# Threshold attention and an ELU feed-forward layer on one core: the score matmuls of full blocks split by halves of the queries

## The chip, the cores and the metric

The kernel runs on one core of a Trainium2 chip. A core has TensorE (PE, matmuls into PSUM), VectorE (DVE), ScalarE (ACT), GpSimd (POOL) and SyncE (SP, which issues most DMAs), each with its own queue of instructions. PSUM has 128 partitions and eight banks of 512 float32 columns.

The metric is the device time of one execution in microseconds. The kernel before has a median of 1265.05 us in three runs, from 1264.96 to 1265.5 us.

## The reference

Batch 8, 8 heads, 576 positions, 64 channels per head; 4608 tokens of 512 channels then go through a layer of 2048 hidden channels. Everything is float32.

```python
scores = scale * np.matmul(q, k.transpose(0, 1, 3, 2))        # (8, 8, 576, 576)
thresh = np.max(scores, axis=-1, keepdims=True) - tau
scores = np.where(scores >= thresh, scores, -1000000000.0)
scores = scores - np.max(scores, axis=-1, keepdims=True)
attn = np.exp(scores)
attn = attn / (np.sum(attn, axis=-1, keepdims=True) + 1e-09)
out = np.matmul(attn, v)                                      # heads side by side: x (4608, 512)
h = x @ w_in
g = np.where(h > 0.0, h, np.exp(np.minimum(h, 0.0)) - 1.0)
return g @ w_out
```

## The kernel before

**Pairs of heads.** Two heads of a batch are one pair, 32 pairs in all. The transposed queries `qT` and keys `kT` of a pair hold head 0 in partitions 0 to 63 and head 1 in partitions 64 to 127, one column per position. A score matmul contracts the 64 channels of one head, so it uses 64 rows of PE's array; which rows follows from the partitions. The 576 queries are four full blocks of 128 (i = 0 to 3, `NC` = 4) and a tail of 64. The queries of a block are the matmul's stationary operand: they are loaded as weights, and come out as the partitions of the scores. The keys stream.

**Early pairs (0 to 3).** `scores` (L479) makes one block of a pair, both heads: for each half of the 576 keys (`HALF` = 288) and each head, one matmul at L493. For the tail (i = NC) it takes `qd`, in which both heads stand in one 128-row operand. `EARLY`, a list written out by hand, gives the order of all tasks up to about 250 us, from the first pairs to pair 8; an entry such as `sc.3` is a call of `scores`, and `wsc.4.0.1` one half of a call of `wide_scores`.

**All other pairs.** `wide_scores` (L751) makes two blocks of a pair, both heads, in one go: four score matrices of 128 by 576, which lie one after another in five PSUM banks (`wide[0]`, the tile `sc`). They are cut where banks end, into eight matmuls at L766, in the order of the tuple `order`: head, block, first column, columns. Head 0 and head 1 alternate, and at no time write the same bank. After one of them ACT copies a column to `seen` (L769). `on_banks` records which engine last touched which bank, and adds the waits that follow: the score matmuls wait for ACT and DVE, which still read the old scores; DVE's maximum (L773), ACT's exponential (L783) and DVE's mask (L787) wait for the matmuls.

**The tail.** `tails_and_values` (L790) makes the scores of the last 64 queries of a pair (L813) beside the first product with the values of the pair two before (L818). Both are matmuls of 64 rows by 64 columns. The rest of the value product follows at L826: 128 rows by 64 columns, one head in each half of the columns.

**The order.** From about 250 us on a planner in the program's builder sets the order. `on_pe(cost, f)` puts PE's work one after another and moves a clock by a fixed cost (2.15 us for `wide_scores`); `at(t, f)` puts the other engines' work at a time. For each pair: `tail_step`, and twice `wide_step` followed by 14 pieces of the feed-forward layer (`ffn_quarters(14)`: L1444 for the first product, L1584 for the second, both matmuls of 128 by 128). After the last pair only feed-forward work is left (L1444, L1958, L2020). The costs only order the work; at run time the engines wait for each other by semaphores.

Of the kernel before, what the change touches and what calls it, by code (L numbers as in the profile page):

```python
# [176 lines left out]
def kernel(  # L177
# [10 lines left out]
    nc = tc.nc  # L188
    PSUM = bass.MemoryType.PSUM
    P = 128  # L190
    B, H, S, D = q.shape
    DM, DF = moe_w_in.shape
    NC = S // P
    MAIN = NC * P
    TAIL = S - MAIN
    HALF = S // 2
# [274 lines left out]
    def vectors(pr):  # L471
        st = {x: small.tile([P, 2], FP32, name=x) for x in ("mx", "th", "su", "rs")}
        st["no"] = step_no[0]
        step_no[0] += 1
        st["sm"] = totals[:, step_no[0] % 6]
        return st


    def scores(pr, i, hs):  # L479
        qT, kT, qd = pairs[pr]  # L480
        if hs[0] == 0:
            open_steps[pr, i] = vectors(pr)
        st = open_steps[pr, i]
        scs = {}
        for h in hs:
            scs[h] = slots[slot_no[0] % 2]
            slot_no[0] += 1
        for a in range(2):
            for h in hs:
                k0 = a * HALF + (0 if h else TAIL)  # L490
                r, qs = (slice(h * D, (h + 1) * D), qT[:, i * P : (i + 1) * P]) if i < NC else (slice(0, P), qd)
                o = scs[h][:, a, :HALF]
                on_banks(nc.tensor.matmul(o, qs[r], kT[r, k0 : k0 + HALF], start=True, stop=True, skip_group_check=True), o)  # L493
        for h in hs:
            st[h] = scs[h]

# [222 lines left out]
    def on_banks(made, ap):  # L719

        ins, needed, starts = made.ins, [], [ap.offset % (5 * 512)]
        for step, n in ap.ap[1:-1]:
            starts = [s + step * k for s in starts for k in range(n)]
        engine = str(ins.engine)
        for x in sorted({b for s in starts for b in range(s // 512, (s + ap.ap[-1][1] - 1) // 512 + 1)}):
            others = [i for e, i in accesses.setdefault(x, []) if e != engine]
            needed += others
            if others and engine == str(nc.tensor.engine):
                accesses[x] = []
            accesses[x].append((engine, ins))  # L730
        needed += [i for y in after[0] for i in banked.get(y, {}).values() if str(i.engine) != engine and i not in needed]
        if doing[0]:
            banked.setdefault(doing[0], {})[engine] = ins
        for other in needed:
            tc.add_manual_dep(ins, other.name,
                              mybir.DependencyInfo(mybir.DependencyClass.Sync, mybir.DependencyReason.DATA), reason="bank")
        for e in (nc.tensor, nc.scalar, nc.vector):
            if str(e.engine) != engine:
                tc.declare_no_dep(ins, group=str(e.engine), keep=needed, reason="other banks")
        tc.add_to_no_dep_group(engine, ins)  # L740
# [5 lines left out]
    def open_step(pr, i, w):  # L746
        st = open_steps[pr, i] = vectors(pr)
        st["w"] = w
        return st

    def wide_scores(pr, half, parts=(0, 1)):  # L751

        qT, kT, _ = pairs[pr]
        for s in range(2) if parts[0] == 0 else ():
            i = 2 * half + s
            st = open_step(pr, i, turned_by[1 - s])
            for h in range(2):
                c = 2 * T + (2 * h + (s ^ h)) * S
                st["sc", h], st["e", h] = wide[0][:, c : c + S], st["w"][:, h * S : (h + 1) * S]
        order = (((0, 0, 0, 448), (1, 1, 0, 320), (1, 1, 320, 256), (0, 0, 448, 128)),  # L760
                 ((1, 0, 0, 256), (0, 1, 0, 384), (1, 0, 256, 320), (0, 1, 384, 192)))
        for h, s, c, n in [x for part in parts for x in order[part]]:
            i, r = 2 * half + s, slice(h * D, (h + 1) * D)
            k0 = c + (0 if h else TAIL)
            o = open_steps[pr, i]["sc", h][:, c : c + n]
            on_banks(nc.tensor.matmul(o, qT[r, i * P : (i + 1) * P], kT[r, k0 : k0 + n], start=True, stop=True,  # L766
                                      skip_group_check=True), o)
            if (h, s, c) == (1, 1, 0):
                on_banks(nc.scalar.copy(seen, o[:, :1]), o[:, :1])  # L769

# [286 lines left out]
    def early_tasks():  # L1057
# [128 lines left out]
        for n in range(per_seq):  # L1186
            pr, i = steps[n]
            hs = heads_of(i)
            masks_a.extend(("mask", n, h) for h in hs)
            job(("sc", n), "pe", lambda e, pr=pr, i=i, hs=hs: scores(pr, i, hs), ("prep", "k", pr, 0), ("copy", "k", pr),  # L1190
                ("prep", "q", pr, int(i > 0)) if i < NC else ("copy", "q", pr), ("sc", n - 1) if n else None, *[masks_a.pop(0) for _ in hs],
                soft=[("norm", n - 4, h) for h in heads_of(steps[n - 4][1])] if n > 3 else ())
# [75 lines left out]
        for z, (pr, what) in enumerate((pr, what) for pr in range(NPAIR, START) for what in ("tail", 0, 1)):  # L1268
            loc = {}
            if what == "tail":  # L1270
                v_ = pr - 2 if pr - 2 >= NPAIR else None
                need_v = [("landed", v_, x) for x in range(NB)] + [("v", v_)] if v_ else []
                job(("tail", pr), "pe", lambda e, pr=pr, v_=v_, loc=loc: loc.update(zip(("main", "outs"), tails_and_values(pr, v_))),
                    *ready_of[pr], *need_v, ("wsc", pr - 1, 1, 1) if pr > NPAIR else "t", *users, soft=steps_b[-4])
                sc_of = {(NC, 0): ("tail", pr)}
                if v_:
                    for part in (1, 0):
                        job(("main", v_, part), "pe", lambda e, part=part, loc=loc: loc["main"](part), ("tail", pr), ("main", v_, 1) if not part else None)
                        job(("outv", v_, part), "act|dve", lambda e, part=part, loc=loc: loc["outs"][part](e), ("main", v_, part))
                group_steps = [(NC, [0], 0)]  # L1280
            else:
                half = what
                for y in range(2):
                    job(("wsc", pr, half, y), "pe", lambda e, pr=pr, half=half, y=y: wide_scores(pr, half, (y,)),
                        ("wsc", pr, half, 0) if y else ("tail", pr) if not half else ("wsc", pr, 0, 1), *ready_of[pr], *users,
                        soft=() if y else steps_b[-4] + steps_b[-3])
                sc_of = {(2 * half + s, h): ("wsc", pr, half, s ^ h) for s in range(2) for h in range(2)}
                group_steps = [(2 * half, [0, 1], 1), (2 * half + 1, [1, 0], 0)]
# [91 lines left out]
    with tc.manual_schedule():  # L1380
# [319 lines left out]
        def wide_step(pr, half):  # L1700
            t = clock[0]
            on_pe(2.15, lambda: wide_scores(pr, half))
            e = t + 2.15
            for s in range(2):
                i = 2 * half + s
                at(e + 1.55 + 1.5 * s, lambda i=i: wide_bounds(pr, i), f"bound{i}")
                for h in range(2):
                    k = 2 * s + (h ^ s)
                    at(e + 0.75 * k, lambda i=i, h=h: wide_max(pr, i, h), f"max{i}{h}")
                    at(e + (1.6, 3.0, 4.7, 5.6)[k], lambda i=i, h=h: wide_exp(pr, i, h), f"exp{i}{h}")  # L1710
                    at(e + (3.0, 4.3, 6.5, 6.9)[k], lambda i=i, h=h: wide_mask(pr, i, h), f"mask{i}{h}")
                finish_of(pr, i, e + (5.1, 7.8)[s], e + (8.4, 10.5)[s])
            if pr + 1 < NP:
                at(e + 5.2, lambda: (prep_k if half else prep_q)(pr + 1), f"prep{half}")
                if not half:
                    at(e + 6.1, lambda: scale_q(pr + 1), "qscale")
                if half:
                    at(e + 6.1, lambda: copy_k(pr + 1), "kcopy")
                    if pr + 2 < NP:
                        at(e + 6.1, lambda: load(pr + 2, ("qm",), True), "loadq")  # L1720
                elif pr > START:
                    at(e + 6.1, lambda: load(pr + 1, ("km",), True), "loadk")
            extras(e + 0.3, e + 1.2, e + 4.2, e + 10.4, e + 12.0)
# [117 lines left out]
        x, y = spaces.popleft(), spaces.popleft()  # L1841
# [5 lines left out]
        a, z = B - 1, B  # L1847
# [281 lines left out]
```

## Time and profile before

| | |
|---|---|
| median of three runs | 1265.05 us (1264.96 to 1265.5) |
| span of the profiled execution, first to last instruction | 1263.4 us |
| PE busy | 1247.3 us, 7163 matmul records |
| PEld (weight loads) busy | 992.0 us, 7163 records |
| DVE, ACT, POOL busy | 1067.8, 584.5, 787.2 us |
| L766 matmul records | 896, 126.5 us busy |
| L493 matmul records with 64 rows | 128, 19.9 us busy |

The profiled execution's own time is known by its span, 1263.4 us; it is 1.65 us under the median of the runs.

How to read it. In a row of groups stand the line, engine, operation, the tiles written and read, the rows and columns of the array in use (64\*128 is 64 rows by 128 columns), the shape that streams, the count, the busy time, the mean duration of one in ns, and then the engine's idle time before them with what ended it. A float32 matmul of the source stands as two MATMUL and two LDWEIGHTS records. Matmuls overlap in the pipeline and their ends are modelled, so a stage is measured here from its first start to the first start of the next stage. In the timeline the first number is the start in us, the second the length, and xN merges N records. In rows of stretches stand the stretch, its length, and for PE, PEld, DVE, ACT and POOL (or those of the line asked for) the busy time and count; then PE's granted clock, the share of the DMA engines and GB/s.

### The profile page before, as it was taken

The page shows a single profiled execution, that of the slowest core. Times are in us where ns is not written, and L with a number is a line of the kernel's source. Part 1 is how long each engine was busy: PE and PEld are TensorE (multiplying, and loading weights), DVE is VectorE, ACT ScalarE, POOL GpSimd, SP SyncE. Part 2 cuts the span into 40 slices and gives each one's busy share as a digit, 9 for nine tenths or more (in the row PEclk, how much of TensorE's full clock was granted, in tenths as well). Part 3 has the DMA queues.
Part 4 walks back from the last instruction along what each step waited for, and adds up shares of the span by engine and source line. Part 5 has one row for each costly group of instructions (what it writes and reads, how often), then busy time and mean ns, then how long its engine had stood idle before and what let it go on. Part 6 is the DMA issues. An engine that isn't in the chain of part 4 may idle for free.

```text
span 1263.4 us, 22606 instructions
## 1 busy us (share of the span) xinstructions
PE 1247.3 (99%) x7163; PEld 992.0 (79%) x7163; DVE 1067.8 (85%) x2322; ACT 584.5 (46%) x1276; POOL 787.2 (62%) x1147
## 2 busy tenths in 40 slices
PE   8999999999999999999999999999999999999998
PEld 6776576588787787878788878778887888899998
DVE  6998989898889879898989888988988885777876
ACT  7987755463434435352625353444535260434130
POOL 5775545586576747574767657675757473675564
PEclk9999999999999999999999999999999999999999
DMA  8468898898989797989989897988898866444433
GB/s 225 147 181 244 217 265 241 241 299 218 263 210 270 217 247 218 263 239 241 238 228 260 225 264 201 274 217 244 216 271 228 236 213 229 156 136 150 142 109 110
DMA packets 332872, 277.71 MB, mean 220 GB/s; under 512 B 201296, under 2 KB 288336, under 8 KB 332752
## 3 DMA queue, kind: packets, MB, share of 16 engines
q1 hardware_dynamic: 331760, 275.73, 78.1%
q8 instruction: 57, 0.93, 0.3%
q10 hardware_dynamic: 992, 0.53, 0.1%
q14 instruction: 63, 0.52, 0.1%
HBM read 178.85 MB, written 97.32 MB: 219 GB/s over the span
## 4 chain that ended last, share of the span: by engine, by line
PE 90%; DVE 4%; DMA 2%; ACT 2%; issue 1%; SPq 0%; POOL 0%; DVEq 0%; ACTq 0%; POOLq 0%
PE f L1444 30%; PE f L1584 23%; PE sc L766 9%; PE sc L826 9%; PE f L1958 4%; PE f L2020 3%; PE f L953 2%; PE f L913 2%; PE sc L493 2%; PE sc L818 1%; PE sc L813 1%; DVE mx L773 1%; PE f L554 1%; PE sc L712 1%; PE f L885 1%
## 5 line engine op out<-in xcount | busy, mean ns | idle before, releaser
L773 DVE TENSOR_REDUCE mx<-sc 128x1 f32<-128x576 f32 x252 | 180.1, 746 | 41.1 <-PE sc L766 34.1
L779 POOL TENSOR_SCALAR th<-mx,ntau 128x2 f32<-128x2 f32 (+1 forms) x140 | 46.0, 329 | 189.9 <-DVE mx L773 189.8
L783 ACT ACTIVATE w_one<-sc,mx 128x576 f32<-128x576 f32 x140 | 100.7, 740 | 132.2 <-DVE mx L773 113.4
L766 PE MATMUL sc<-kT,qT 64*128 64x256 f32 (+5 forms) x896 | 126.5, 418 | 2.1 <-ACT xt L432 0.9
L787 DVE SCALAR_TENSOR_TENSOR w_one<-sc,th,w_one 128x576 f32<-128x576 f32 x140 | 109.9, 812 | 20.4 <-ACT w_one L783 19.7
L766 PEld LDWEIGHTS sc<-kT,qT 64*128 64x128 f32 x896 | 99.3, 186 | 35.4 <-issue 18.9
L1444 PE MATMUL f<-xt,sw 128*128 128x256 f32 x512 | 123.7, 384 | 1.3 <-DMA sw<-win_sums 0.8
L1444 PE MATMUL f<-x,w_in_sb 128*128 128x256 f32 x512 | 122.8, 382 | 0.0
L783 ACT ACTIVATE e<-sc,mx 128x576 f32<-128x576 f32 x112 | 82.7, 742 | 86.1 <-DVE mx L773 84.5
L1444 PE MATMUL f<-xt,w_in_sb 128*128 128x256 f32 x512 | 121.2, 379 | 0.5 <-DVE xt L1053 0.5
L501 POOL TENSOR_SCALAR w_one<-w_one,rs 128x576 f32<-128x576 f32 x115 | 89.4, 787 | 38.9 <-DVE rs L551 38.9
L640 DVE STREAM_TRANSPOSE x<-w_one 128x512 f32<-128x512 f32 (+1 forms) x140 | 99.9, 743 | 13.5 <-POOL w_one L501 7.6
L1444 PEld LDWEIGHTS f<-xt,sw 128*128 128x128 f32 x512 | 94.1, 190 | 20.2 <-issue 4.3
L1444 PEld LDWEIGHTS f<-x,w_in_sb 128*128 128x128 f32 x512 | 96.2, 190 | 16.1 <-ACT g L1505 3.6
L1444 PEld LDWEIGHTS f<-xt,w_in_sb 128*128 128x128 f32 x512 | 97.2, 190 | 14.0 <-ACT e L783 0.8
L787 DVE SCALAR_TENSOR_TENSOR e<-sc,th,e 128x576 f32<-128x576 f32 x112 | 87.6, 807 | 8.3 <-ACT e L783 7.9
L1584 PE MATMUL f<-w_out_sb,g 128*128 128x256 f32 x384 | 92.0, 382 | 0.0
L1584 PE MATMUL f<-w_out_sb,s 128*128 128x256 f32 x384 | 91.9, 382 | 0.0
L1584 PE MATMUL f<-t,s 128*128 128x256 f32 x384 | 90.7, 379 | 0.0
L1584 PEld LDWEIGHTS f<-w_out_sb,g 128*128 128x128 f32 x384 | 72.0, 190 | 12.2 <-issue 2.9
L1584 PEld LDWEIGHTS f<-w_out_sb,s 128*128 128x128 f32 x384 | 71.9, 190 | 12.0 <-issue 2.5
L1584 PEld LDWEIGHTS f<-t,s 128*128 128x128 f32 x384 | 73.0, 190 | 9.9
(344 smaller groups left out, 2887.6 us busy)
## 6 DMA issues: line engine op xcount, KB each, us to landing
there<-x SPq DMA_DIRECT2D x452, 144.0 KB, 3.8
wTb<-there SPq DMA_DIRECT2D x58, 576.0 KB, 6.2
wTa<-there SPq DMA_DIRECT2D x55, 576.0 KB, 4.3
sw<-win_sums SPq DMA_DIRECT2D x62, 384.0 KB, 4.2
t<-wout_sums SPq DMA_DIRECT2D x45, 512.0 KB, 5.2
there<-x SPq DMA_DIRECT2D x112, 80.0 KB, 1.9
wTb<-there SPq DMA_DIRECT2D x56, 160.0 KB, 3.8
wst<-in_moe_w_in_dram SPq DMA_DIRECT2D x16, 512.0 KB, 4.7
```

The source lines that it names most:

```text
L501: nc.gpsimd.tensor_scalar(wv, wv, st["rs"][:, h : h + 1], 1.0, ALU.mult, ALU.mult)
L640: nc.vector.transpose(x[:, :, c0 : c0 + nc_], src.rearrange("p (c g n) -> p g c n", c=nc_, n=T))
L766: on_banks(nc.tensor.matmul(o, qT[r, i * P : (i + 1) * P], kT[r, k0 : k0 + n], start=True, stop=True, skip_group_check=True), o)
L773: on_banks(nc.vector.tensor_reduce(st["mx"][:, h : h + 1], st["sc", h], axis=AX.XY if i == NC else AX.X, op=ALU.max, negate=True), st["sc" ...
L779: nc.gpsimd.tensor_scalar(st["th"][:, cs], st["mx"][:, cs], -1.0, ntau, ALU.mult, ALU.add)
L783: on_banks(nc.scalar.activation(st["e", h], st["sc", h], AF.Exp, bias=st["mx"][:, h : h + 1]), st["sc", h])
L787: on_banks(nc.vector.scalar_tensor_tensor(st["e", h], st["sc", h], st["th"][:, h : h + 1], st["e", h], ALU.is_ge, ALU.mult, accum_out=st[" ...
L826: on_banks(nc.tensor.matmul(o, vm[:, h, c], parts[part][:, g0:g1, h * (NC + 1) + c], start=False, stop=(c == NC - 1), skip_group_check=Tru ...
L1444: nc.tensor.matmul(loc["banks"][place], left[:, j], right[:, j], start=(begins and j == 0), stop=(j == 1), skip_group_check=True)
L1584: nc.tensor.matmul(place(m), lhs, rhs, start=(begins and v == 0), stop=(v == RU - 1), skip_group_check=True)
L1958: nc.tensor.matmul(loc["x"][place][:, :P], left[:, v], right[:, v], start=(begins and v == 0), stop=(v == 1), skip_group_check=True)
L2020: nc.tensor.matmul(loc[c][:, :HM], lefts(g, r, c, m)[:, v], rights(r, m)[:, v], start=(v == 0), stop=(v == RU - 1), skip_group_check=True)
```

## The change

In `scores` and `wide_scores` each matmul of a full block becomes two. The stationary operand is 64 queries in place of 128, and the output is the lower or the upper 64 partitions of the same columns of PSUM. The keys that stream are the same for both. The second follows right behind the first. The tail of `scores` keeps its one matmul of 128 rows. What is computed, and where it lies, stays the same.

```diff
@@ scores
-                o = scs[h][:, a, :HALF]
-                on_banks(nc.tensor.matmul(o, qs[r], kT[r, k0 : k0 + HALF], start=True, stop=True, skip_group_check=True), o)
+                for y in range(2 if i < NC else 1):
+                    oy = scs[h][y * D : (y + 1) * D, a, :HALF] if i < NC else scs[h][:, a, :HALF]
+                    on_banks(nc.tensor.matmul(oy, qs[r, y * D : (y + 1) * D] if i < NC else qs[r], kT[r, k0 : k0 + HALF], start=True, stop=True, skip_group_check=True), oy)
@@ wide_scores
             o = open_steps[pr, i]["sc", h][:, c : c + n]
-            on_banks(nc.tensor.matmul(o, qT[r, i * P : (i + 1) * P], kT[r, k0 : k0 + n], start=True, stop=True,
-                                      skip_group_check=True), o)
+            for y in range(2):
+                oy = o[y * D : (y + 1) * D]
+                on_banks(nc.tensor.matmul(oy, qT[r, i * P + y * D : i * P + (y + 1) * D], kT[r, k0 : k0 + n], start=True, stop=True,
+                                          skip_group_check=True), oy)
             if (h, s, c) == (1, 1, 0):
                 on_banks(nc.scalar.copy(seen, o[:, :1]), o[:, :1])
```

## The prediction

> **What bounds the kernel now.** I read the page first: its engine line, its slices and its chain.
>
> ```profile
> span 1263.4 us, 22606 instructions
> ...
> PE 1247.3 (99%) x7163; PEld 992.0 (79%) x7163; DVE 1067.8 (85%) x2322; ACT 584.5 (46%) x1276; POOL 787.2 (62%) x1147
> ...
> PEclk9999999999999999999999999999999999999999
> ...
> q8 instruction: 57, 0.93, 0.3%
> ...
> PE 90%; DVE 4%; DMA 2%; ACT 2%; issue 1%; SPq 0%; POOL 0%; DVEq 0%; ACTq 0%; POOLq 0%
> PE f L1444 30%; PE f L1584 23%; PE sc L766 9%; PE sc L826 9%; PE f L1958 4%; PE f L2020 3%; PE f L953 2%; PE f L913 2%; PE sc L493 2%; PE sc L818 1%; PE sc L813 1%; DVE mx L773 1%; PE f L554 1%; PE sc L712 1%; PE f L885 1%
> ```
>
> TensorE (PE) is busy for 99% of the span at the full granted clock, and 90% of the chain that ended last is PE. A busy PE does not say that it is full, so I then asked for stretches, for all engines, and in a second question for the score line L766 alone.
>
> ```profile
> 0.00:125.00 125.00, 116.75 (x880) 88.39 (x881) 106.15 (x235) 103.47 (x222) 78.34 (x123) 1.00 0.73 197
> 125.00:255.00 130.00, 128.15 (x624) 77.82 (x622) 117.02 (x251) 76.20 (x146) 70.37 (x101) 1.00 0.90 243
> 255.00:960.00 705.00, 704.53 (x3957) 567.03 (x3956) 619.00 (x1364) 310.40 (x681) 461.93 (x696) 1.00 0.89 241
> ```
>
> ```profile
> 0.00:125.00 125.00, 2.48 (x16) 1.83 (x16) 1.00 0.73 197
> 125.00:255.00 130.00, 22.34 (x144) 16.54 (x144) 1.00 0.90 243
> 255.00:960.00 705.00, 92.86 (x672) 73.87 (x672) 1.00 0.89 241
> 960.00:1071.00 111.00, 8.84 (x64) 7.04 (x64) 1.00 0.75 231
> ```
>
> From 255 to 960 us the first busy column (PE) has 704.53 of 705 us. The longest wait of PE on anything after 255 us is one of 0.8 us:
>
> ```profile
> PE f L1444 <- DMA sw<-win_sums: 0.8, 1, 0.8
> ```
>
> So a microsecond that a score stage gains or loses there moves the end by a microsecond. Before 255 us the other engines are on the chain too. Now the stage itself, in the timeline of PE:
>
> ```profile
> 406.67 2.21 PE L766 MATMUL sc<-kT,qT 64*128 64x448 f32 x16
> 408.81 1.99 PE L1444 MATMUL f<-xt,sw 128*128 128x256 f32 x8
> ...
> 421.24 0.45 PE L813 MATMUL sc<-kT,qT 64*64 64x288 f32 x1
> 421.25 0.43 PE L818 MATMUL sc<-wTa,vd 64*64 64x256 f32 x1
> 421.25 0.45 PE L813 MATMUL sc<-kT,qT 64*64 64x288 f32 x1
> 421.26 0.48 PE L818 MATMUL sc<-wTb,vd 64*64 64x320 f32 x1
> 421.51 0.38 PE L818 MATMUL sc<-wTa,vd 64*64 64x256 f32 x1
> ...
> 422.37 2.37 PE L826 MATMUL sc<-wTb,vm 128*64 128x320 f32 x16
> 424.58 1.90 PE L826 MATMUL sc<-wTa,vm 128*64 128x256 f32 x16
> 426.40 2.21 PE L766 MATMUL sc<-kT,qT 64*128 64x448 f32 x16
> 428.54 1.99 PE L1584 MATMUL f<-w_out_sb,g 128*128 128x256 f32 x8
> 430.37 1.89 PE L1584 MATMUL f<-t,g 128*128 128x256 f32 x8
> 432.10 1.89 PE L1584 MATMUL f<-w_out_sb,g 128*128 128x256 f32 x8
> ```
>
> Starts are what counts here, since ends are modelled. Eight matmuls in the source give 16 records: each float32 matmul runs as two passes. From 430.37 to 432.10 eight records of 256 columns take 1.73 us, 0.216 us each, so a pass streams a column in 0.844 ns.
>
> A stage of L766 lasts 408.81 - 406.67 = 2.14 us, and the next one, 428.54 - 426.40, the same. Each head's row group streams 448 + 128 + 384 + 192 = 1152 columns in two passes: 2304 x 0.844 = 1.944 us. Were the two heads taken in turn it would be 3.89 us, so they already run side by side and the 128 rows are full. What is left, 2.14 - 1.944 = 0.196 us, is the start of the stage. These rows split it (the first line of each pair of counts is minimum, median, maximum in ns):
>
> ```profile
> L766 PE MATMUL sc<-kT,qT x16: 269/402/640, 406.7 to 408.6; 64*128 64x320 f32 x4, 64*128 64x256 f32 x4, 64*128 64x448 f32 x2, 64*128 64x128 f32 x2
> L766 PE MATMUL sc<-kT,qT 64*128 64x448 f32 x2 | 1.0, 588 | 0.0
> L813 PE MATMUL sc<-kT,qT x8: 402/402/453, 421.2 to 422.0; 64*64 64x288 f32 x8
> ...
> L766 PEld LDWEIGHTS sc<-kT,qT 64*128 64x128 f32 x896 | 99.3, 186 | 35.4 <-issue 18.9 <-ACT seen L769 2.5 <-ACT xt L432 1.9
> ...
> L813 PEld LDWEIGHTS sc<-kT,qT 64*64 64x64 f32 x224 | 14.2, 132 | 12.9 <-issue 6.0 <-POOL u L1463 3.3 <-ACT xs L432 1.5
> ```
>
> Of the two 448-column passes the first takes 640 ns, so the second takes 2 x 588 - 640 = 536: the first waits 0.104 us for its 128 columns of weights, which nothing covers. The remaining 0.092 us is the change of array shape.
>
> **The change part by part.**
>
> *The streaming.* Each of the eight matmuls becomes two of half the queries. A tile of 64 by 64 streams the same keys, so 1152 columns in two passes, 1.944 us, on each of four tiles. If the four run side by side, the stage streams as long as before: nothing is gained and nothing lost. The trace shows four such tiles in the tail stage (L813 and L818): the four first starts lie within 421.24 to 421.26 us, and the stage lasts 422.37 - 421.24 = 1.13 us for 576 columns in two passes per tile, which is 0.972 us of streaming. In sequence it would be twice that.
>
> *The start of the stage.* The weights are 64 columns in place of 128. The L813 row gives that start: 453 - 402 = 0.051 us in place of 0.104. The tail stage has 1.13 - 0.972 - 0.051 = 0.107 us left, where the wide stage has 0.092: 0.015 us for the later starts of the third and fourth tile. New stage: 1.944 + 0.051 + 0.107 = 2.102 us, 0.038 us less. Bounds: 0.053 less if the late starts cost nothing; 0.023 less if the 0.015 us doubles with twice the passes. I take 0.038, since it is the measured stage plus streaming alone.
>
> *How often.* 896 records are 56 stages of L766. From 255 us on there are (672 + 64) / 16 = 46, all in the stretch where PE waits for nothing: 46 x 0.038 = 1.75 us. Before it lie (16 + 144) / 16 = 10, and they are longer:
>
> ```profile
> 121.31 2.52 PE L766 MATMUL sc<-kT,qT 64*128 64x448 f32 x16 [0.33 <-DVE w_one L787]
> ...
> 148.43 2.52 PE L766 MATMUL sc<-kT,qT 64*128 64x448 f32 x16
> ...
> L493 PE MATMUL sc<-x 64*128 64x288 f32 x64 | 10.0, 427 | 1.0 <-DVE w L537 0.8
> L493 PE MATMUL sc<-kT,qT 64*128 64x288 f32 x64 | 9.9, 428 | 1.1 <-DVE w L537 0.6 <-DVE w_one L537 0.5
> ...
> 72.37 1.20 PE sc L493 x8
> ...
> 180.25 5.97 DMA wTb<-there
> ```
>
> There the two halves of the stage are separate tasks, 2.52 against 2.21 us, and the second half starts anew, so the start is saved twice: 20 x 0.038 = 0.76 us. The 128 records of L493 with 64 rows are 16 stages of 8, each with one start: 0.61 us. These 1.37 us count only where the chain passes there. It does through many of them (the row at 72.37), but it also takes DMA steps of 6 us (180.25). I take two thirds, 0.9 us; the bounds are none and all.
>
> *What comes with it.* PE gets 1024 more LDWEIGHTS and 1024 more MATMUL records, 14% of its 14326. Queue q8, which carries instructions, grows from 57 packets by about 8; its share is 0.3%, and the cover is that they are fetched ahead. Were that gone, each would stop PE for its landing. The order of all engines stays as it was. The second half-matmul has no wait of its own, since it writes the bank that the first has just waited for. ACT's copy of one column (`seen`, L769) waits for both halves and, in 14 places, for an earlier instruction of ACT; ACT is 46% busy, so I cost that at nothing. The maxima, exponentials and masks read the same banks about 0.04 us earlier, and nothing is queued differently behind them.
>
> *The sum.* 1.75 + 0.9 = 2.65 us less. The profiled span of 1263.4 us lies 1.65 us under the median of the runs, 1265.05; what lies around the span stays. Forecast: 1265.05 - 2.65 = 1262.4 us. With the bounds: 46 x 0.023 = 1.1 us gained at least, 1264.0; at most (46 + 20 + 16) x 0.053 = 4.3 us, 1260.7.
>
> **The rivals.**
>
> *The early part gives nothing.* Only the 46 late stages count: 1.75 us, 1263.3, within 0.2% (2.53 us, about what a measurement of this kernel can tell from no change). For it speaks the 180.25 row; against it that PE is busy for 245 of the first 255 us.
>
> *Slower: passes start in the order of the program.* Then a matmul's second pass, on the same tile, holds back the next tile's first one. The stage is the sum over all 16 matmuls of one pass each, 4608 columns x 0.844 = 3.89 us, and the last pass, 0.16: 4.05 in place of 1.94 us of streaming, 56 x 2.1 = 118 us, 1383. It decides once a stage loses more than the 0.053 us of its start. Against it: by strict order the third start in the tail stage would lie one pass, 0.24 us, behind the first, and it lies 0.01 behind. This order is a rule of the Trainium skill, TensorE: Matmul & The Clock Gate, "What overlaps and what doesn't" in Part 3: matmuls start and end strictly in program order, and only weight loads are pulled ahead. By that rule the stage would be the 4.05 us; the four starts here disagree, so it gets a small chance, for a look-ahead that is shorter than eight halves in a row need.
>
> *Slower: PE cannot take instructions so fast.* The new stage needs 32 matmuls in 2.10 us, 15.2 per us. The nearest rows are the tail stage, 16 in 1.13 us (14.2 per us), and this one, 16 in 1.03 us:
>
> ```profile
> 46.47 1.09 PE L712 MATMUL sc<-wTb,vm 128*64 128x128 f32 x16
> 47.50 0.65 PE L554 MATMUL f<-ident,w 128*128 128x128 f32 x4
> ```
>
> Both are limited by their streaming, and both are half as long. At 14.2 per us the stage takes 2.25 us, 0.11 more than before: 56 x 0.11 = 6.2 us, 1271. It decides below 32 / 2.14 = 15.0 per us.
>
> **How the numbers follow.** That four tiles run side by side at full rate: 0.82. Inside it the gain passes 2.53 us if the early part keeps over 57% of its 1.37 us: 0.45 faster, 0.37 within 0.2% (the first rival among them). Instruction rate: 0.09, slower. Program order: 0.06, slower. Some other contention, such as two tiles reading the same key rows at once: 0.03, of which 0.01 is too small to tell. Together: faster 0.45, same 0.38, slower 0.17. The forecast's own range is 1260.7 to 1264.0; I reach up to 1265.5, where a lost start takes all the gain, and leave the slower rivals out.
>
> **What would show it.** In the profile after: 8187 matmuls; L766's records doubled to 1792, all 64\*64, their weight loads near 132 ns; 2.10 us from the first L766 start to the next stage's start; four starts within 0.02 us; L826 and L1444 as before; the shapes' changes still 0.09 us. A stage over 2.14 us, first starts that lie a pass apart, or idle time before L766 put down to issue would make the prediction wrong.

## The result, and the profile after

The changed kernel takes 1263.47 us (median of 21 runs, 1262.13 to 1264.42) against 1265.19 us for the kernel before in the same measurement (21 runs, 1264.51 to 1266.74). The ratio is 0.9987 with a 95% interval of 0.9981 to 0.9992: 1.72 us, or 0.13%, less. That is inside the predicted range (1260.7 to 1264.0), but the forecast's own 2.65 us lies outside the interval, which is 1.0 to 2.4 us, and the change is within the 0.2% called no change. The number is the first rival's 1263.3 almost to the digit; whether its mechanism is too is taken up below. Five lines of the page of the changed kernel:

```profile
span 1261.1 us, 24668 instructions
PE 1245.4 (99%) x8187; PEld 970.9 (77%) x8187; DVE 1068.6 (85%) x2322; ACT 584.7 (46%) x1276; POOL 788.6 (63%) x1147
q8 instruction: 65, 1.06, 0.3%
PE 82%; DVE 3%; issue 1%; ACT 0%; DMA 0%; SPq 0%; POOL 0%; DVEq 0%; ACTq 0%
PE f L1447 30%; PE f L1587 23%; PE sc L829 9%; PE sc L769 8%; PE f L1961 4%; PE f L2023 3%; PE sc L821 1%; PE f L888 1%; PE sc L816 1%; DVE mx L776 1%; PE f L956 1%; DVE x L641 1%; DVE e L790 0%; DVE w_one L790 0%; DMA there<-x 0%
```

The matmul records are 8187 and q8 has 65 packets, as the prediction counted. The weight loads' busy time falls although there are 1024 more of them. The late stages, in the timeline of PE of the changed kernel (line L766 is L769 now):

```profile
254.86 2.17 PE L769 MATMUL sc<-kT,qT 64*64 64x448 f32 x32
...
278.56 2.25 PE L1447 MATMUL f<-xt,sw 128*128 128x256 f32 x8
280.65 1.03 PE L1447 MATMUL f<-x,sw 128*128 128x256 f32 x4
...
285.06 0.45 PE L816 MATMUL sc<-kT,qT 64*64 64x288 f32 x1
...
406.56 2.17 PE L769 MATMUL sc<-kT,qT 64*64 64x448 f32 x32
408.66 0.70 PE L1447 MATMUL f<-xt,sw 128*128 128x256 f32 x2
...
426.25 2.17 PE L769 MATMUL sc<-kT,qT 64*64 64x448 f32 x32
428.35 0.92 PE L1587 MATMUL f<-w_out_sb,g 128*128 128x256 f32 x3
```

From first start to the next stage's first start it is 408.66 - 406.56 = 2.10 us, and 428.35 - 426.25 = 2.10, where the kernel before had 2.14. Over all 46 stages from 254 us on the median falls by 0.040 us (2.141 to 2.101); 45 of them take 2.10 to 2.12 us, and one, at 970 us, takes 2.42. The rows of the stage itself, of its longest passes and of the weight loads:

```profile
L769 PE MATMUL sc<-kT,qT x32: 269/402/587, 406.6 to 408.4; 64*64 64x320 f32 x8, 64*64 64x256 f32 x8, 64*64 64x448 f32 x4, 64*64 64x128 f32 x4
L769 PE MATMUL sc<-kT,qT 64*64 64x448 f32 x4 | 1.0, 562 | 0.0
L769 PEld LDWEIGHTS sc<-kT,qT 64*64 64x64 f32 x1792 | 80.7, 132 | 48.3 <-issue 18.2 <-ACT seen L772 3.3 <-ACT xt L432 1.9
```

The longest first pass is 587 ns in place of 640, so the uncovered weights went from 0.104 to 0.051 us. The four first starts are merged to one row if a very short stretch of the same timeline is shown, 0.59 us long with its 587 ns passes; all four start within 0.02 us:

```profile
406.56 0.59 PE L769 MATMUL sc<-kT,qT 64*64 64x448 f32 x4
```

Where the time went is read best from four starts: the first block of L493, the first wide stage, the first late wide stage (254 to 256 us), and the first tail matmul behind it (L813, now L816). All in us, each kernel from one profiled execution:

| kernel | first L493 | to first wide stage | to first late stage | to tail | tail starts at |
|---|---|---|---|---|---|
| before | 7.07 | 114.23 | 133.76 | 29.84 | 284.91 |
| changed | 7.54 | 114.04 | 133.28 | 30.20 | 285.06 |

From the tail stage to the end of the scores (the last L766 record, L769 now), which holds 44 of the 46 late stages, the changed kernel needs 735.71 us against 738.21. Of these 2.50 us, 0.8 is one DMA wait of the profiled execution of before (the 0.8 us row of the prediction); the rest, 1.7, is the late stages' own, 44 x 0.04. Two profiles of unsplit late stages without that wait, from the experiments below, take 737.40 us here, and five of kernels with split late stages take 735.67 to 735.71.

At 285 us the changed kernel is not ahead: 285.06 against 284.91. From the first block to the first late stage it gains 0.19 + 0.48 = 0.67 us. The stretch from 255 to 285 us is then 0.36 us longer, though it holds two stages that are each 0.04 shorter, and its first block starts 0.47 us later. Counted from the first block, 0.31 us are left. In these profiles the first block starts anywhere from 7.07 to 8.11 us, and no run shows whether the change has a part in that.

### The profile page after: what moved, and what is told of

It is laid out like the page before. It is cut to its first block, busy times and chain, and to the rows that moved or that the text cites. A ratio compares the mean times of both kernels' runs of the same rounds, so it can differ in the third digit from the quotient of the medians.

```text
span 1261.1 us, 24668 instructions
## 1 busy us (share of the span) xinstructions
PE 1245.4 (99%) x8187; PEld 970.9 (77%) x8187; DVE 1068.6 (85%) x2322; ACT 584.7 (46%) x1276; POOL 788.6 (63%) x1147
## 4 chain that ended last, share of the span: by engine, by line
PE 82%; DVE 3%; issue 1%; ACT 0%; DMA 0%; SPq 0%; POOL 0%; DVEq 0%; ACTq 0%
PE f L1447 30%; PE f L1587 23%; PE sc L829 9%; PE sc L769 8%; PE f L1961 4%; PE f L2023 3%; PE sc L821 1%; PE f L888 1%; PE sc L816 1%; DVE mx L776 1%; PE f L956 1%; DVE x L641 1%; DVE e L790 0%; DVE w_one L790 0%; DMA there<-x 0%
## 5 line engine op out<-in xcount | busy, mean ns | idle before, releaser
L769 PE MATMUL sc<-kT,qT 64*64 64x256 f32 (+5 forms) x1792 | 124.2, 410 | 2.4 <-DVE su L546 0.5
L769 PEld LDWEIGHTS sc<-kT,qT 64*64 64x64 f32 x1792 | 80.7, 132 | 48.3 <-issue 18.2
L502 POOL TENSOR_SCALAR e<-e,rs 128x576 f32<-128x576 f32 x92 | 67.8, 742 | 20.8 <-DVE rs L552 18.3
```

The source lines that it names most:

```text
L502: nc.gpsimd.tensor_scalar(wv, wv, st["rs"][:, h : h + 1], 1.0, ALU.mult, ALU.mult)
L769: on_banks(nc.tensor.matmul(oy, qT[r, i * P + y * D : i * P + (y + 1) * D], kT[r, k0 : k0 + n], start=True, stop=True, skip_group_check=Tr ...
```

## The experiments

Two theories stood against each other at first: that four tiles run side by side and the stage saves half of its uncovered weight load, which is worth its size wherever PE is what the end waits for (A); and that the time comes from elsewhere, or that the passes' order or the instruction rate decides (the prediction's rivals). For the stretch from 255 to 285 us, theory C is that full DMA engines take back what the part before has gained.

### Late stages alone, early stages alone

The late stages are those in which the planner calls `wide_scores` with both halves; the hand-written list calls it with one. The first kernel splits only the former (`scores` as before). The second splits only the early work: `scores` as in the changed kernel, and `z = P if len(parts) == 2 else D`. The first one's edit, shortened at the dots:

```diff
+            z = D if len(parts) == 2 else P
+            for y in range(P // z):
+                oy = o[y * z : (y + 1) * z]
+                on_banks(nc.tensor.matmul(oy, qT[r, i * P + y * z : i * P + (y + 1) * z], kT[r, k0 : k0 + n], ...), oy)
```

> Only the 46 wide stages that the planner places (from about 250 us on) are split; the ten earlier ones and the blocks of the first four pairs are as before. Theory A (each late stage gives its 0.040 us, as the trace of the changed kernel shows, and the early split gives nothing): 46 x 0.040 = 1.84 us under the kernel before, about 1263.4 us, as much as with the whole change. Rival B (the early split gives its 0.9 us, and waits that come new after 255 us take it back): about 0.9 us under before, 1264.3 us.

> The other part alone: the blocks of the first four pairs and the ten wide stages before about 250 us are split, the 46 late ones are not. Theory A: no difference, within 0.3 us of before. Rival B: 0.7 to 1.4 us under before. In the trace the first late stage shows the gain of the early part by its start, 255.07 us in the kernel before.

Measured: late alone 1263.31 against 1265.33 us, ratio 0.9983 (0.9974 to 0.9992), 2.02 us less. So the late stages alone give what the whole change gives, as A said. Early alone 1264.46 against 1265.33, ratio 0.9992 (0.9983 to 1.0). By its median that is 0.87 us less, which is what B expected (0.7 to 1.4) and not A (0.3 at most); but the interval goes from 0 to 2.1 us and decides neither. That the two gains add up is not what the whole change shows, 1.72 us against 2.02 + 0.87.

The trace of early alone keeps both gains up to the first late stage (114.06 and 133.29 us for the two intervals, where the kernel before has 114.23 and 133.76), and loses them right behind it: its stretch to the tail takes 31.08 us instead of 29.84. From the waits of its trace between 255 and 290 us:

```profile
PE f L1448 <- DVE xt L1057: 1.1, 1, 1.1
```

In the kernel before this wait is 0.47 us, so 0.64 of the 1.24 us lie here. The other 0.60 lie in the first late stage, which takes 2.75 us and in which PE waits for ACT's copy into `xs`. This execution took 1265.61 us, the second slowest of its eleven, so it shows that the gain can be lost, and not how much of it the median loses.

### All wide stages without L493, and the changed kernel again

The third kernel splits all 56 wide stages and leaves `scores` as before (the edit against the changed kernel, shortened at the dots):

```diff
-                for y in range(2 if i < NC else 1):
-                    ...
+                o = scs[h][:, a, :HALF]
+                on_banks(nc.tensor.matmul(o, qs[r], kT[r, k0 : k0 + HALF], ...), o)
```

> All 56 wide stages split, early and late; the blocks of the first four pairs (L493) as before. From the traces: 46 x 0.040 = 1.84 us and 0.48 us between the first wide stage and 255 us, 2.3 us under the kernel before, about 1262.9. If the split of L493 costs as much as it gives (four of its 16 stages follow a turn of the tail in the shape 64 by 128, and now have a change of shape between them), this kernel is equal to the changed one or up to 0.5 us faster; if L493 gives its 0.2 to 0.6 us, it is slower by that.

> The changed kernel once more, on the same chip as the run with the wide stages alone. Theory A: 2.3 to 2.6 us under the kernel before by its traces (1.84 late, 0.48 early wide stages, 0.0 to 0.2 L493); its own first measurement gave 1.72 us with an interval of 1.0 to 2.4. A gain under 1.8 us here too would say that something behind the stages takes back part of what they give.

Measured on one chip: 1263.69 us without L493 (ratio 0.9989, 0.998 to 0.9997) and 1263.46 with it (0.9986, 0.9977 to 0.9995), before 1264.97. The intervals overlap, so the medians can't price L493. The traces can, up to the first wide stage: without the split of L493 its stretch takes 114.23 us as before, and with it 114.05. Sixteen stages give 0.18 to 0.19 us and no more. Both kernels gain less than the 2.3 us and more that the traces up to 255 us and the late stages had promised: 1.28 us (interval 0.4 to 2.5) and 1.51 (0.6 to 2.9). By the expectation's own mark of 1.8 us something takes part of the gains back, but the intervals don't exclude 2.3.

The second profile of the changed kernel shows where an execution can lose time. It took 1265.63 us, the slowest of its eleven. The first late stage starts at 255.72 us there, and the tail stage at 287.85, 32.13 us later instead of 29.84. Its timeline (rows of DVE, ACT and PE, with the idle time before each in brackets), and then its waits between 255 and 290 us:

```profile
272.68 1.44 DVE L641 STREAM_TRANSPOSE x<-w_one 128x640 f32<-128x640 f32 x2 [3.06 <-DMA there<-x]
274.05 0.39 DVE L1469 TENSOR_TENSOR g<-f,t 128x256 f32<-128x256 f32 x1
...
274.52 0.63 ACT L1477 ACTIVATE ge<-g 128x512 f32<-128x512 f32 x1 [2.36 <-DVE g L1469]
...
273.49 2.12 PE L1447 MATMUL f<-xt,sw 128*128 128x256 f32 x8 [0.37 <-DMA sw<-win_sums]
280.38 1.13 PE L1447 MATMUL f<-x,w_in_sb 128*128 128x256 f32 x4 [0.87 <-ACT g L1508]
```

```profile
DVE x L641 <- DMA there<-x: 3.1, 1, 3.1
PEld f L1447 <- DMA sw<-win_sums: 0.7, 1, 0.7
```

DVE's transpose waits for an earlier transfer to leave the tile `x`. Behind it in DVE's queue stands the sum `g` (L1469), which ACT waits for (2.36 us), and PE then waits for ACT. The chain of what ended last shows the same. Rows of it from the kernel before, where it is PE alone from 261.40 us on, then from the first and the second profile of the changed kernel:

```profile
261.40 9.01 PE f L1444 x40
...
272.56 12.43 PE f L1444 x56
```

```profile
265.36 4.42 DMA there<-x
...
279.68 5.45 PE f L1447 x24
```

```profile
266.01 6.55 DMA there<-x
```

So in the changed kernel the chain goes through the last of four transfers to `there` and then through DVE. In the kernel before that transfer took 3.71 us. But does the wait come from what the split gained ahead of it? All in us, one profile each:

| kernel | first late stage at | DVE's wait for `there` | to the tail |
|---|---|---|---|
| before | 255.07 | 0.5 | 29.84 |
| changed | 254.86 | 1.1 | 30.20 |
| changed again | 255.72 | 3.1 | 32.13 |
| late alone | 255.36 | 1.4 | 30.46 |
| early alone | 255.22 | none | 31.08 |
| without L493 | 254.94 | 1.8 | 30.88 |

Late alone has gained nothing up to its first late stage, and still loses 0.70 us here (30.46 against 29.84 less 2 x 0.04). The execution that comes last, at 255.72 us, waits longest. The same kernel waits 1.1 us in one execution and 3.1 in another. So these waits differ from execution to execution, and that an earlier PE makes them longer isn't shown.

### The stores moved out of that stretch

At the start of the planner's part SP issues three stores of 0.5 MB each (`wout_sums`), planned 6 us apart. The DMA engines are full around them. In stretches of PE, the last two columns are the DMA engines' share and GB/s; first the kernel before, then the changed one:

```profile
270.00:275.00 5.00, 5.00 (x30) 1.00 1.04 385
270.00:275.00 5.00, 5.00 (x46) 1.00 1.05 370
```

They are as full in the kernel before, which lost nothing there in its profile.

The edit issues these stores 24 us later, once in the changed kernel and once in the kernel before:

```diff
-                    at(t + 7.0 + 6.0 * x, lambda x=x: nc.sync.dma_start(wout_sums[0, x], ...))
+                    at(t + 31.0 + 6.0 * x, lambda x=x: nc.sync.dma_start(wout_sums[0, x], ...))
```

> The changed kernel with the three stores of 0.5 MB into wout_sums issued 24 us later in the first planned pair, past the stretch of 260 to 280 us. Theory C (in that stretch the DMA engines are full, the stores of turned weights land late, DVE and then PE wait, and what the early stages had gained is lost there): DVE's wait for the DMA of there between 262 and 290 us goes from 1.1 and 3.1 us to under 0.5, the time from the first late wide stage to the tail stage behind it shrinks from 30.2 to 29.8 us or less, and the kernel takes 0.4 to 1.0 us less than the changed one, 1262.5 to 1263.1. Rival (the waits come from chance in the loads and not from what is issued there): waits and time as in the changed kernel, 1263.5.

> The kernel before with the same three stores moved. Theory C: before the change PE came later and lost nothing there in its profile, so at most 0.3 us less, 1264.8 to 1265.2. Rival: no difference, or 0.4 us and more gained here as well, which would say that the crowd of DMAs is not the change's doing.

Measured: the changed kernel 1262.57 us (1262.14 to 1263.97), ratio 0.9984 (0.9975 to 0.9993), against 1264.73 for before; the kernel before with the same edit 1264.62, ratio 0.9998 (0.9989 to 1.0007). The changed kernel with later stores, the same stretch and the timeline of PE:

```profile
270.00:275.00 5.00, 5.00 (x46) 1.00 0.94 263
```

```profile
255.11 2.17 PE L769 MATMUL sc<-kT,qT 64*64 64x448 f32 x32
...
278.73 1.89 PE L1447 MATMUL f<-xt,sw 128*128 128x256 f32 x8
280.46 1.03 PE L1447 MATMUL f<-x,sw 128*128 128x256 f32 x4
...
284.87 0.45 PE L816 MATMUL sc<-kT,qT 64*64 64x288 f32 x1
```

From the first late stage to the tail it is now 29.76 us, which is the 29.84 of before less 2 x 0.04, and DVE's wait for `there<-x` isn't in the trace of that stretch. PE's eight matmuls at 278.73 us take 1.73 us to the next row, where the changed kernel takes 2.09. The numbers are those that C expected; the reason that it gives is not what this trace shows. The last transfer to `there` takes 4.38 us, as long as the 4.42 of the changed kernel's first profile. What changed is when it is issued, 264.31 us instead of 265.36. In SP's queue, where issues follow one another, the first store stood ahead of it. Rows of SP, from the changed kernel and then from the one with later stores:

```profile
260.17 0.42 SPq L1768 DMA_DIRECT2D wout_sums<-t  x1
...
263.98 1.83 SPq L660 DMA_DIRECT2D there<-x  x4
```

```profile
262.93 1.84 SPq L660 DMA_DIRECT2D there<-x  x4
```

With the stores moved the four transfers to `there` went about a microsecond earlier, half of which is the store's own place in the queue (the next issue follows it at 260.68 us), and they landed before DVE came to its transpose. Why the same transfer took 6.55 us in the changed kernel's second profile stays open: from 265 to 270 us the DMA share is 0.93 there, and 0.93 and 0.94 in the first profiles of before and changed.

The rival, chance in the loads, is not excluded either: early alone doesn't wait for `there` in this stretch, with the stores where they were. For the kernel before the edit does nothing: its tail starts 29.84 us after its first late stage with it too. In time the effect isn't shown. The median of 1262.57 us is the lowest of all kernels, but the ratio to before, 0.9984, lies in the intervals of the changed kernel's two measurements (0.9987 and 0.9986), and late alone, with the stores in place, has 0.9983.

### Lower halves first, upper halves behind

The two halves of a matmul stand side by side in PE's queue in the changed kernel. Here all lower halves of a part come first:

```diff
-        for h, s, c, n in [x for part in parts for x in order[part]]:
+        for y, (h, s, c, n) in [(y, x) for part in parts for y in range(2) for x in order[part]]:
...
-            if (h, s, c) == (1, 1, 0):
+            if (y, h, s, c) == (1, 1, 1, 0):
```

> The same halves in another order: within each half of a stage all four matmuls of the lower queries first, then the four of the upper queries. The first upper half then stands 16 records of PE behind the first lower one. Theory A (PE looks past passes that must wait, at least that far): stage of 2.10 us as in the changed kernel, the four first starts within 0.03 us, time about 1263.4. Rival (PE looks ahead only a few records, and the changed kernel profits from its order): only two tiles run until the lower halves are under way, a stage between 2.5 and 4.0 us, time 1285 to 1370.

Measured: 1295.69 us, one run. The time and the stages lie where the rival had them, but not for its reason, as the first row below shows. A wide stage takes 2.61 us in 23 of the 46 late places and 2.90 to 2.98 in the others. Its timeline, where the first row is from a very short stretch and the last is ACT's; then, from the view of the copy's line, who waited for it (us in all, times):

```profile
415.20 0.61 PE L768 MATMUL sc<-kT,qT 64*64 64x448 f32 x4
415.20 2.68 PE L768 MATMUL sc<-kT,qT 64*64 64x448 f32 x32
417.81 0.48 PE L1446 MATMUL f<-xt,sw 128*128 128x256 f32 x1
416.48 0.16 ACT L771 COPY seen<-sc 128x1 f32<-128x1 f32 x1 [1.93 <-PE sc L768]
```

```profile
  PEld sc L768: 9.9, 32
  PE sc L768: 2.9, 10
```

The first upper half stands 16 records behind the first lower half, and still the four first starts lie within 0.034 us, in the one row of four. By starts in strict order, as the Trainium skill has it (TensorE: Matmul & The Clock Gate, "What overlaps and what doesn't" in Part 3), the upper halves would start behind all 16. The trace disagrees, and with it falls the rival's reason, that only two tiles run at first. What makes the stage longer is the copy to `seen`: in this order the 192-column matmul of the second part, whose bank the copy reads, comes ahead of the upper halves, so PE's queue stands until the copy has ended (416.48 + 0.16; the next weight load is at 416.69), and with it all that is behind.

The test of that: the same order, with the last matmul of each part moved behind the upper halves.

```diff
+        ... for part in parts for g in ((0, 3), (3, 4)) for y in range(2) for x in order[part][g[0] : g[1]]
```

> The halves still apart, but the last matmul of each half of the stage, 192 columns of head 0 in the bank that ACT's copy to seen guards, comes behind the upper halves. Theory A (in the run with the halves apart, PE's queue stood behind this one wait for ACT's copy, and PE's look-ahead was not the limit): stages back to 2.10 us, four first starts within 0.03 us, about 1263.5 us. Rival (too short a look-ahead): stages still 2.5 us and more, 1285 us or above.

Measured: 1276.36 us, one run. 35 of the 46 late stages now take 2.15 us:

```profile
412.14 2.22 PE L768 MATMUL sc<-kT,qT 64*64 64x448 f32 x32
414.30 0.91 PE L1446 MATMUL f<-xt,sw 128*128 128x256 f32 x3
```

The ten early ones take 2.61 to 2.67 us, and there PE still waits for `seen`, in every one. The other 11 late ones take 2.32 to 2.74 us without that wait; in the one at 362.98 us PE's next weight load, at 363.52, comes behind ACT's copy into `xt`, which ends at 363.47. One matmul moved out of the copy's way has brought back 1295.69 - 1276.36 = 19 of the 32 us, so the wait was the main cause. The 0.05 us by which 2.15 misses the expected 2.10 isn't settled.

### Quarters: 32 columns of queries

Four matmuls of 64 by 32 for each of the old ones, in the late stages (`z = T if len(parts) == 2 else D`).

> The 46 late stages in four matmuls of 32 queries each (tiles of 64 by 32), the earlier ones in halves. Theory A (the start of a stage is its uncovered weight load, and each further tile starts 0.007 us later): 1.944 of streaming + 0.092 + 0.026 for 32 columns of weights + about 0.05 for eight starts = 2.11 us, so nothing more is gained, about 1263.5 us. Rival (the start does not depend on the columns of the weights but halved for another reason): 2.13 us and more. Rival (PE can not take 64 matmuls in 2.1 us, or eight tiles do not run side by side): stages of 2.5 us or more, 1285 us and above.

Measured: 1264.92 us, one run, stages of 2.15 us in place of the expected 2.11. The first row is the stage's source view, the others the timeline:

```profile
L770 PE MATMUL sc<-kT,qT x64: 268/403/561, 406.8 to 408.7; 64*32 64x320 f32 x16, 64*32 64x256 f32 x16, 64*32 64x448 f32 x8, 64*32 64x128 f32 x8
```

```profile
406.78 2.22 PE L770 MATMUL sc<-kT,qT 64*32 64x448 f32 x64
408.94 0.48 PE L1448 MATMUL f<-xt,sw 128*128 128x256 f32 x1
```

The stage is as long as the rival had it whose start doesn't depend on the columns of the weights (2.13 us and more), but that isn't the reason. The start fell as A expected: the longest first pass is 561 ns, so the weights cost 561 - 536 = 0.025 us. The time is lost in the middle of the stage. The second part's first weight loads come at 407.75 us, 64 records after the stage's first; in the four tiles of head 0 its matmuls then start 0.03 to 0.06 us after the passes before them have streamed their columns, and their first passes take 504 ns where the second ones take 483. Why they come late isn't known.

### Only the first matmul of each head in halves

In the late stages only the two matmuls whose weights nothing covers are split; the six others stay 64 by 128 (`z = D if len(parts) == 1 or (h, s, c) in ((0, 0, 0), (1, 1, 0)) else P`).

> In the 46 late stages only the first matmul of each head (448 and 320 columns) is split in halves; the other six are 128 queries wide as before. Theory A (the start of a stage is the uncovered weight load of its first shape, and a change of shape costs a drain, a start of its own and the uncovered load again): the stage begins 0.05 us faster, then changes shape: + 0.092 + 0.104, and the two heads no longer end the first shape together, 448 against 320 columns in two passes, 0.2 us; a stage of 2.4 to 2.5 us, about 1278 us. Rival (64 by 64 and 64 by 128 share the row tiles and need no drain between them): 2.10 us, about 1263.4 us.

Measured: 1279.97 us, one run, at the upper end of what A expected for the stage (2.4 to 2.5 us):

```profile
409.33 2.56 PE L770 MATMUL sc<-kT,qT 64*64 64x448 f32 x20
411.83 1.35 PE L1448 MATMUL f<-xt,sw 128*128 128x256 f32 x5
```

411.83 - 409.33 = 2.50 us. Going from 64\*64 to 64\*128 inside the stage costs what the stage's start costs again. The last 64\*64 pass starts at 0.434 us of the stage and streams its 448 columns in 0.378; the first 64\*128 pass starts at 0.900, 0.09 us later. And 0.104 us of weights are covered by nothing: of the first matmul's two 64\*128 passes of 256 columns the one takes 480 ns, the other 376. The rest of the 0.40 us is that heads with unequal ends wait for each other: head 1 is through with its 320 columns 0.2 us before head 0 with its 448. The Trainium skill says that a switch of the tiling mode has to drain the array (TensorEngine Tiling (Array Packing), Key Properties); this trace agrees, with the 0.09 us between the end of the streaming and the first new start, and the two numbers are the price of one such switch.

## Why the prediction was right, and which step failed

**The streaming.** Right. Four tiles of 64 by 64 stream side by side, and the stage is as long as its 1.944 us and its start. Neither strict order nor the instruction rate (32 matmuls in 2.10 us, 15.2 per us) holds it up; in quarters 64 matmuls went through in 2.15 us, 29.8 per us.

**The start of the stage, and the late term.** Right in size: 2.101 us measured against 2.102, 46 x 0.040 = 1.84 us against 1.75. The late stages alone give it all on the chip (2.02 us, interval 1.0 to 3.3). Behind 285 us the gain moves the end, as the prediction said of all that lies after 255 us: against the profile of the kernel before with later stores, 43 of the 45 distances from one late stage to the next are 0.02 to 0.05 us shorter. One is equal, and one, from 270 to 290 us, is 0.40 longer.

**The early term: the step that failed.** It was 0.9 us, two thirds of 1.37, taken by the chain of waits. The traces show 0.67 us at the first late stage. Beside the late stages' 1.84 us the interval of the whole change, at most 2.4 us, leaves 0.6 at the end; the second measurement, with fewer runs, leaves 1.1. The range held all the same, because it had been drawn from none to all of this term; that the total came out inside it says nothing for the two thirds.

- The sizes. Up to the first late stage the ten wide stages gave 0.48 us instead of up to 0.76, and the 16 stages of L493 0.19 instead of up to 0.61. It is not the single stage that was mis-sized: twelve of the 16 fall from 1.17 to 1.13 us, by 0.040 where 0.038 was predicted. For the other four one cause is seen. In the kernel before, L493 with its 64\*128 follows the turn L405, which is 64\*128 too, so there is no change of shape to pay; halves of 64\*64 bring one in. Timelines, before and changed:

```profile
11.56 0.27 PE L405 MATMUL f<-ident,w_out_sb 64*128 64x64 f32 x1
11.72 1.24 PE L493 MATMUL sc<-x 64*128 64x288 f32 x8
12.90 0.33 PE L554 MATMUL f<-ident,w_out_sb 128*128 128x128 f32 x1
```

```profile
12.07 0.27 PE L405 MATMUL f<-ident,w_out_sb 64*128 64x64 f32 x1
12.27 1.20 PE L494 MATMUL sc<-x 64*64 64x288 f32 x16
13.40 0.33 PE L555 MATMUL f<-ident,w_out_sb 128*128 128x128 f32 x1
```

  The stage itself falls from 1.18 to 1.13 us, but from L405 to it 0.16 has become 0.20. Four stages follow L405; in one of them, at 16.3 us, PE waits before it in both kernels, and nothing is lost. How the twelve lose most of their 0.5 us before the first wide stage isn't taken apart.

- The way to the end. Of the 0.67 us at the first late stage, 0.44 (0.36 + 2 x 0.04) are lost between 255 and 285 us in the changed kernel's first profile, more in its second, and none with later stores. There the sentence that a microsecond gained after 255 us moves the end by one, read off the small waits of PE in the kernel before, doesn't hold: the chain goes through a transfer, DVE and ACT. But late alone loses 0.70 us there too, with nothing gained ahead. How much of the 0.67 us reaches the end of a median execution stays open.

**The rival whose number came out.** The early part gives nothing, 1263.3 us. It was argued with the DMA steps on the chain around 180 us; the runs show the gain still there at 255 us, so for that reason it is wrong. That its number fits so well is partly luck: the interval of the whole change leaves the early part anything up to 0.6 us, and early alone has a median of 0.87.

**What comes with it.** 1024 more records of each kind cost nothing seen: q8's 8 more packets, its share of 0.3%, and the order of the engines are as predicted. The copy to `seen`, costed at nothing, is that only in this order: with the halves apart the wait for it was worth about 19 us, the difference of two single runs.

## What to carry to other kernels

Here every row group of the array was already in use. Cutting the columns too gave no more streaming, only half of the one weight load that nothing covered, and one change of tile shape more in the stage took away several times that. What a part upstream gains has to be followed to the end, stretch by stretch: small waits of the engine that bounds the kernel, read in one execution, don't show that a stretch lets the gain through, since the same kernel waited 1.1 us there in one execution and 3.1 in the next. Look up first whether the profiled execution was a fast or a slow one among its runs. And when an instruction is cut in two, its halves are best kept side by side in the queue: with the halves apart, one that waited for a semaphore held up all that stood behind it.

## What was not expected of the hardware

- PE started passes ahead of others in its queue over a longer way than the tail stage had shown: an upper half started 0.034 us after the first lower one with 16 records between them (415.20 us, halves apart). It did not pass an instruction that waited for a semaphore: the next weight load came at 416.69 us, when the copy had ended.
- In quarters the matmuls of head 0 started 0.03 to 0.06 us late in the middle of the stage, behind 64 records in a row (407.75 us). The cause is open.
- A change of shape took about 0.09 us both at a stage's start and in its middle, and the uncovered weights cost 0.104, 0.051 and 0.025 us for 128, 64 and 32 columns.
- The same transfer to `there` took 3.71 us from issue to landing in the kernel before, and 4.42 and 6.55 us in two executions of the changed one, at the same DMA share of 0.93 to 0.94 between 265 and 270 us.
